# First-batch k and v loads in four 64x64 quarters, paired q tails, and two parameter rows spread by DMA, in a fused attention and MLP kernel

## The chip, the cores and the metric

The kernel runs on one core of one Trainium2 chip. The metric is the device time of one execution in microseconds. Engines are named as in the profile: PE (matrix products), ACT, DVE and POOL (elementwise work), SP (here only the issue of DMAs).

## The reference

Linear attention without a softmax over 8 batches, 8 heads, 576 rows and head size 64, an RMS norm per head, then a mixing block over tokens and channels (width 512, hidden width 2048):

```python
kv = einsum('bhsd,bhse->bhde', k, v)
out = einsum('bhsd,bhde->bhse', q, kv)
x = out / sqrt(mean(out * out, -1) + 1e-6) * g_norm      # heads are then put side by side: (8, 576, 512)
a1 = alpha1 * x + beta1
u = x + lam * einsum('ts,bsd->btd', w_tok, a1)           # token mix
a2 = alpha2 * u + beta2
y = u + lam * (relu(a2 @ w_ch1) @ w_ch2)                 # channel mix
```

All inputs and the output are float32.

## The kernel before

The work of a batch is cut into chunks of 128 rows (four, and a tail of 64). For each batch PE makes k-v products (L674, L684), q-kv products (L765 and L390), the token mix (L854, tails L876), the first channel product (L988 for even batches, L1002 for odd ones, 16 groups with a relu on ACT, L979) and the second (L1024). Between q-kv and token mix stands the norm: a square on ACT (L800), then on DVE a reduce (L802), a reciprocal (L808), a scaling of the result in PSUM (L821) and a product that makes the token mix's operand `rt`, or `rtt` for the tail (L825); POOL multiplies by g_norm (L829).

The first batch is done in another way, in fp32 straight from the loaded tiles, so that PE can start before everything is split into bf16 pairs: k-v products at L610 (`kv_first`), q turned by PE at L632 (main part) and L646 (the 64-row tails), both in `qt_first`, and q-kv products at L772, all in two halves of four heads. L906 is its token mix in halves. The loads of that batch (`load_first` for k and v, L510; L494 and L501 for q) stand first on SP's queue, then w_tok (L1118), the first-matrix weights (L1240) mixed with batch 1's k, v and q, and the second-matrix weights (L1263), one after the other (`P.chain`).

The weights of the second matrix are multiplied by lambda when they are cast (L1269, on DVE or POOL), so `lam_bc`, lambda on all 128 partitions, must be there by then. `a2_bc`, alpha2 on all partitions, is used from the third batch on. These, `e1g_bc` (alpha1 times lambda times g_norm) and `g_bc` are made by a matmul with a row of ones (L1096, `spread`) and a copy.

No engine's order is written by hand. Every operation is recorded with an estimated cost, and for DMAs a transfer time (`dma_us`); `plan` then simulates the queues and fixes each engine's order, choosing priorities so that the first 16 first-channel groups come early. Until the first of them starts, PE gets a filling matmul (L1330, `warm`) wherever the plan finds nothing ready; their number and places are fixed with the order. PSUM has eight banks, which the plan hands out too; a q-kv group of two chunks takes two neighbouring ones until DVE has scaled it. So a changed cost or operation can move instructions anywhere.

Of the kernel before, what the change touches and what calls it, by code (L numbers as in the profile page):

```python
# [17 lines left out]
DM = 512  # L18
# [30 lines left out]
class Prog:  # L49
# [119 lines left out]
    def schedule(self):  # L169
# [226 lines left out]
def bass_transnormer_attn__then__resmlp_affine_kernel(  # L396
# [15 lines left out]
    with ExitStack() as stack:  # L412
# [80 lines left out]
        def load_main(tile, key, src, b, hs, eng="SP"):  # L493
            P.op(eng, 0.6, lambda e: e.dma_start(  # L494
                tile[:, hs].rearrange("p h c d -> p h (c d)"),
                src[b, hs, 0:512, :].rearrange("h (p c) d -> p h (c d)", c=4)),
                w=[(key, a) for a in range(hs.start // 4, hs.stop // 4)],
                dma_us=3.6 * (hs.stop - hs.start) / 8)

# [8 lines left out]
        def load_first(a):  # L508
            for key, src, tile in (("kf", k, kf), ("vf", v, vf)):
                P.op("SP", 0.6, lambda e, src=src, tile=tile: e.dma_start(  # L510
                    six(tile, a).rearrange("p h c d -> p h (c d)"),
                    src[0, HALVES[a], :, :].rearrange("h (p c) d -> p h (c d)", c=6)),
                    w=[(key, a)], dma_us=2.05)

        def load_kv(b, go=()):
            j = (b + 1) % 2
            for tile, tl, src, n in ((kf, kft, k, "kf"), (vf, vft, v, "vf")):
                P.op("SP", 0.6, lambda e, tile=tile, src=src: e.dma_start(
                    tile[:, j].rearrange("p h c d -> p h (c d)"),
                    src[b, :, 0:512, :].rearrange("h (p c) d -> p h (c d)", c=4)),  # L520
                    r=go, w=[(n, j)], dma_us=3.6)
# [77 lines left out]
        def kv_first():  # L599

            def group(a):
                t = P.ptile(1)

                def f(e):
                    ks, vs = six(kf, a), six(vf, a)
                    for c in range(6):
                        for h in range(4):
                            o = t.flat(slice(64 * (h % 2), 64 * (h % 2) + 64))[
                                :, 64 * (h // 2):64 * (h // 2) + 64]
                            m = e.matmul(o, ks[:, h, c, :], vs[:, h, c, :],  # L610
                                         start=(c == 0 and h < 2), stop=(c == 5),
                                         skip_group_check=True)
                    return m
                P.op("PE", 1.7, f, r=[("kf", a), ("vf", a)], w=[t])
                for h in range(2):
                    rows = slice(64 * h, 64 * h + 64)
                    P.op("ACT", act_us(128), lambda e, h=h, rows=rows: copy(
                        e, kv32[rows, 2 * a:2 * a + 2, 64 * h:64 * h + 64],
                        t.flat(rows)[:, 0:128].rearrange("p (r e) -> p r e", r=2)),
                        r=[t, "kvz"], w=[("kv32", a, h)])  # L620
            for a in range(2):
                yield lambda a=a: group(a)

        def qt_first():

            def pair(pr):
                t = P.ptile(1)

                def f(e):
# [5 lines left out]
                    return m  # L635
                P.op("PE", 1.0, f, r=["ident", ("qf", pr // 2)], w=[t])
                P.op(act_dve(512), 0, lambda e: copy(e, qt32[:, pr, 0:512], t.flat()),
                     r=[t], w=[("q32", pr)])

            def tail(a):  # L640
                t = P.ptile(1)

                def f(e):
                    for pr in range(2):
                        for h in range(2):
                            m = e.matmul(t.flat(slice(64 * h, 64 * h + 64))[  # L646
                                :, 64 * pr:64 * pr + 64], qft[0:64, 4 * a + 2 * pr + h, :],
                                ident[0:64, 0:64], start=True, stop=True)
                    return m
                P.op("PE", 0.4, f, r=["ident", "qft0"], w=[t])  # L650
                P.op(act_dve(128), 0, lambda e: copy(
# [362 lines left out]
        def ch2_groups(b):  # L1014
# [31 lines left out]
            for c, n in order:  # L1046
# [4 lines left out]
        abr = xtl[0:8, 1, 64:192]  # L1051
        params = ((moe_lam, prow[:, 512:1024], lam_bc, "lam"),
                  (moe_alpha1, prow[:, 0:512], e1g_bc, "e1"), (g_norm, prow2[:, 0:64], g_bc, "g"),
                  (moe_beta1, prow[:, 1024:1536], None, "e2"),
                  (moe_alpha2, prow[:, 1536:2048], a2_bc, "a2"))

# [9 lines left out]
        def load_params():  # L1066
            t = P.ptile(1)
            P.op("PE", 0.1, lambda e: e.transpose(t.flat()[:, 0:8], abr[0:8, :], ident[0:8, 0:8]),
                 r=["ident", ("abr", 0), ("abr", 1)], w=[t])
            P.op("DVE", 0.2, lambda e: e.tensor_copy(  # L1070
                out=ab2[:].rearrange("p i j -> p (i j)"), in_=t.flat()[:, 0:8]),
                r=[t], w=[("ab2", 0)])
            P.op("DVE", 0.2, lambda e: e.tensor_copy(out=b2c[:], in_=t.flat()[:, 4:8]),
                 r=[t], w=["b2c"])
            e1r, lamr, e2r, gr = (params[i][1] for i in (1, 0, 3, 2))
# [11 lines left out]
            spread(("e1", "g"))  # L1087

        def spread(names):
            late = [] if "g" in names else [("wtm", sc) for sc in range(5)]  # L1090
            for src, row, dst, key in params:
                if key not in names:
                    continue
# [3 lines left out]
                    t.flat()[:, 0:n], ones[:], row, start=True, stop=True),  # L1097
                    r=["ones", key + "r"] + late, w=[t])
                P.op(act_dve(n), 0, lambda e, dst=dst, t=t, n=n: copy(
                    e, dst[:], t.flat()[:, 0:n]), r=[t], w=[key])  # L1100

        def free_rows():
            for kk in (xkeys(1, c) for c in range(4)):
                for x_ in kk:
                    for key in ("e1r", "lamr", "e2r", "a2r"):
                        P.readers.setdefault(x_, []).extend(P.readers[key] + P.lastw[key])
# [113 lines left out]
        run([wt_groups()])  # L1220
        spread(("lam", "a2"))
        free_rows()
# [57 lines left out]
        load_q(1)  # L1280
        load_w(3)
        P.chain = False
        for key in ("wst", "wst2", "hsu"):
# [8 lines left out]
        for i in range(4, 8):  # L1292
            load_w(i)
        P.chain = False

# [67 lines left out]
```

## Time and profile before

| | us |
|---|---|
| median of 3 runs | 373.29 |
| lowest and highest | 373.05, 374.56 |
| profiled execution, its own time | 372.88 |
| its span in the profile | 371.1 |
| PE busy in the span | 359.2 (97%) |
| DVE, ACT, POOL busy | 197.0, 166.2, 79.9 |

The mean granted PE clock is 0.999. All times in the rows below are microseconds from the start of the span unless marked ns. A row of the timeline gives start, length, engine, line, operation, result and operands, shapes, a count of instructions, and in brackets how long the engine was idle before and what ended that. An fp32 matmul appears as two records. The chain of waits is the work that ended last, followed backwards. A row of the table by stretches gives the length, the busy time and count of PE, PEld (weight loads), DVE, ACT and POOL, then the granted clock, the DMA share and GB/s. Transfers stay in flight after the SP row that issued them. Matmuls overlap, so several PE rows together are timed from start to start.

### The profile page before, as it was taken

How to read it: one execution, taken by the hardware profiler on the slowest of the kernel's cores; microseconds unless marked ns; L12 is line 12 of the kernel's file. 1: busy time of each engine (PE TensorE's matmuls, PEld its weight loads, DVE VectorE, ACT ScalarE, POOL GpSimd, SP SyncE). 2: the span in 40 equal slices, each digit the busy share in tenths (PEclk: the TensorE clock that was granted, in tenths of full speed). 3: DMA queues.
4: the chain of work that ended last, by engine and by line, in shares of the span. 5: the costliest groups of instructions: out<-in, count | busy, mean ns of one | idle time of the engine just before them, and what ended most of it. 6: DMA issues, size and time to landing. Idle time of an engine off the chain costs nothing.

```text
span 371.1 us, 6911 instructions
## 1 busy us (share of the span) xinstructions
PE 359.2 (97%) x3074; PEld 208.9 (56%) x2838; DVE 197.0 (53%) x300; ACT 166.2 (45%) x268; POOL 79.9 (22%) x69
## 2 busy tenths in 40 slices
PE   7999999999999999999999999999999999999995
PEld 3887665466654554457664554457654554457642
DVE  3267598976566467834836166924833175720021
ACT  1466797217862088206670087207730186007500
POOL 4046008520242005300242006200520006100000
PEclk9999999999999999999999999999999999999999
DMA  8999999989969399439923399423503110330021
GB/s 191 252 349 296 327 384 300 265 195 253 282 130 226 110 300 225 54 115 260 245 51 86 127 306 185 76 101 58 113 8 107 58 30 1 66 114 5 2 83 58
DMA packets 92456, 59.33 MB, mean 160 GB/s; under 512 B 59454, under 2 KB 83526, under 8 KB 92298
## 3 DMA queue, kind: packets, MB, share of 16 engines
q1 hardware_dynamic: 92400, 58.88, 63.1%
q8 instruction: 23, 0.38, 0.4%
q14 instruction: 7, 0.06, 0.0%
q10 hardware_dynamic: 26, 0.01, 0.0%
HBM read 38.04 MB, written 9.44 MB: 128 GB/s over the span
## 4 chain that ended last, share of the span: by engine, by line
PE 88%; DMA 4%; DVE 4%; ACT 1%; issue 1%; SPq 1%
PE ps L1024 30%; PE ps L1002 18%; PE ps L988 14%; PE ps L854 8%; PE ps L674 4%; DMA qf<-in_q_dram 4%; PE ps L390 2%; PE ps L765 2%; PE ps L876 1%; PE ps L906 1%; PE ps L941 1%; DVE small L802 1%; DVE rt L825 1%; PE ps L684 1%; SPq L510 1%
## 5 line engine op out<-in xcount | busy, mean ns | idle before, releaser
L1024 PE MATMUL ps<-w,ht 128*128 128x512 bf16 x551 | 126.0, 379 | 2.5 <-issue 1.7
L979 ACT ACTIVATE ht<-ps,hb 128x512 bf16<-128x512 f32 (+1 forms) x128 | 93.4, 742 | 46.0 <-PE ps L1002 38.8
L1024 PEld LDWEIGHTS ps<-w,ht 128*128 128x128 bf16 x576 | 54.5, 98 | 64.1 <-issue 1.2
L829 POOL TENSOR_TENSOR xm<-xm,g_bc 128x512 f32<-128x512 f32 (+1 forms) x36 | 46.4, 1288 | 190.3 <-DVE rt L825 188.4
L1002 PE MATMUL ps<-a2t,w 128*128 128x320 bf16 x512 | 72.0, 299 | 0.5 <-ACT ht L979 0.5
L1002 PEld LDWEIGHTS ps<-a2t,w 128*128 128x128 bf16 x512 | 49.2, 98 | 21.6 <-ACT ht L979 1.3
L988 PE MATMUL ps<-a2t,w 128*128 128x512 bf16 x246 | 57.0, 379 | 0.6 <-issue 0.2
L1033 DVE TENSOR_TENSOR xm<-ps,xm 128x512 f32<-128x512 f32 x32 | 22.1, 689 | 63.6 <-PE ps L1024 63.4
L701 ACT ACTIVATE kvd<-ps 64x128 bf16<-64x128 f32 x28 | 7.6, 272 | 86.0 <-PE ps L684 85.6
L988 PEld LDWEIGHTS ps<-a2t,w 128*128 128x128 bf16 x256 | 23.9, 98 | 26.3
L802 DVE TENSOR_REDUCE small<-sq 128x16 f32<-128x1024 f32 (+3 forms) x27 | 25.3, 936 | 23.6 <-ACT sq L800 23.6
L861 DVE TENSOR_TENSOR xm<-ps,xm 128x1024 f32<-128x1024 f32 x14 | 17.0, 1220 | 21.8 <-PE ps L854 21.8
L854 PE MATMUL ps<-rt,wt 128*128 128x512 bf16 x106 | 27.5, 379 | 0.4 <-DVE rtt L825 0.2
L800 ACT ACTIVATE sq<-ps 128x1024 f32<-128x1024 f32 (+3 forms) x27 | 21.6, 798 | 6.7 <-PE ps L772 3.5
L562 DVE TENSOR_TENSOR qs<-qf,qs 128x2048 bf16<-128x2048 f32 (+1 forms) x10 | 16.4, 1659 | 9.4 <-ACT qs L490 9.3
L706 DVE TENSOR_TENSOR kvd<-ps,kvd 64x128 bf16<-64x128 f32 x28 | 8.1, 289 | 25.0 <-ACT kvd L701 24.4
L765 PEld LDWEIGHTS ps<-kvd,qt 128*128 128x128 bf16 x280 | 17.9, 98 | 4.2
L821 DVE TENSOR_TENSOR xm<-ps,small 128x1024 f32<-128x1024 f32 (+1 forms) x18 | 19.7, 1098 | 0.4
L825 DVE TENSOR_TENSOR rt<-xm,e1g_bc 128x1024 bf16<-128x1024 f32 (+1 forms) x17 | 19.4, 1140 | 0.2
L490 ACT ACTIVATE qs<-qf 128x2048 bf16<-128x2048 f32 (+1 forms) x8 | 12.7, 1588 | 14.9 <-DMA qf<-in_q_dram 12.3
L390 PE MATMUL ps<-kvd,qt 128*128 128x64 bf16 x280 | 19.2, 193 | 0.0
L765 PE MATMUL ps<-kvd,qt 128*128 128x64 bf16 x280 | 19.1, 193 | 0.0
(107 smaller groups left out, 293.0 us busy)
## 6 DMA issues: line engine op xcount, KB each, us to landing
out_dram<-xm SPq DMA_DIRECT2D x32, 256.0 KB, 2.4
kf<-in_k_dram SPq DMA_DIRECT2D x7, 1024.0 KB, 9.5
vf<-in_v_dram SPq DMA_DIRECT2D x7, 1024.0 KB, 7.3
qf<-in_q_dram SPq DMA_DIRECT2D x7, 1024.0 KB, 8.7
stg<-in_moe_w_ch_dram SPq DMA_DIRECT2D x3, 1024.0 KB, 12.3
kf<-in_moe_w_ch_dram SPq DMA_DIRECT2D x2, 1024.0 KB, 14.5
kf<-in_k_dram SPq DMA_DIRECT2D x2, 576.0 KB, 8.4
vf<-in_v_dram SPq DMA_DIRECT2D x2, 576.0 KB, 10.4
```

The costliest lines, as they stand in the source:

```text
L390: return pe.add_instruction(mybir.InstMatmult(start_tensor_calc=start, stop_tensor_calc=stop, tile_size=(128, 128), tile_position=(0, 0), ...
L765: e.matmul(o, w, kvd[:, h, 0, :], start=True, stop=False)
L800: P.op("ACT", act_us(64 * m), lambda e: e.activation(sqv, raw(), ACT.Square), r=[t], w=[("sq", sqs)])
L802: P.op("DVE", dve_us(64 * m), lambda e: e.tensor_reduce(out=smv, in_=sqv.rearrange("p (h d) -> p h d", h=m), axis=AX.X, op=ALU.add), r=[(" ...
L825: lambda e: e.tensor_tensor(out=r_, in0=x, in1=eb, op=ALU.mult),
L829: P.op("POOL", pool_us(64 * nh), lambda e, xc=xc: e.tensor_tensor(out=xc, in0=xc, in1=g_bc[rows, None, :].to_broadcast([nr, nh, DH]), op=A ...
L854: m = e.matmul(t.ap()[:, i, :], tok_w(b, sc, c), rsrc(b, sc), start=(sc == 0), stop=(sc == 4))
L979: P.op("ACT", act_us(n) + 0.09, lambda e: e.activation(dst, src(), ACT.Relu, bias=hb[:, fj:fj + 1]), r=[t, ("hb", fj // 4)], w=[("ht", fj)])
L988: m = e.matmul(t.flat(), w1[:, dj, 128 * fj:128 * fj + 128], a2t[:, dj, 0:512], start=(dj == 0), stop=(dj == 3))
L1002: m = e.matmul(t.ap()[:, i, 0:320], w1[:, dj, 128 * fj:128 * fj + 128], a2t[:, dj, 320 * i:320 * i + 320], start=(dj == 0), stop=(dj == 3))
L1024: m = e.matmul(t.flat(), ht[:, fj, 128 * c:128 * c + 128], w2[:, fj, :], start=(fj == 0), stop=(fj == 15))
L1033: P.op("DVE", dve_us(512), lambda e: e.tensor_tensor(out=x, in0=t.flat(), in1=x, op=ALU.add), r=[t] + keys, w=keys)
```

## The change

1. The first batch's k and v. A half of four heads was one DMA onto 96 partitions of 6 rows; it becomes two DMAs of two heads each onto partitions 0 to 63 and 64 to 127, with 9 rows (2304 bytes) to a partition. The k-v products of a half then are 36 matmuls of 64x64, spread over the four quarters of PE, instead of 24 of 96x64.
2. The q tails of the first batch: two heads are turned at once by one transpose, four in all instead of eight matmuls.
3. lambda and alpha2 are spread over the partitions by a DMA that reads the row 128 times, instead of by PE (L1096) and a copy on ACT. The lambda load stands on SP's queue behind the fourth weight load, the alpha2 load behind the eighth. The small row load of alpha2 goes away.
4. Costs that the plan uses are changed: 4.2 instead of 3.6 us for a q load, 3.8 instead of 3.6 for a batch's k or v, 0.6 instead of 0.3 from issue to start of a transfer, and PE times of the operations above.

```diff
-                        dma_free = max(dma_free, t + 0.3) + pick.lat
+                        dma_free = max(dma_free, t + 0.6) + pick.lat
...
-        def six(tile, a):
-            return tile[0:96, a].rearrange("p h c d -> p (h c d)")[:, 0:1536].rearrange(
-                "p (h c d) -> p h c d", h=4, c=6)
+        def nine(tile, a, g):
+            return tile[64 * g:64 * g + 64, a].rearrange("p h c d -> p (h c d)")[
+                :, 0:1152].rearrange("p (h c d) -> p h c d", h=2, c=9)
...
         def load_first(a):
             for key, src, tile in (("kf", k, kf), ("vf", v, vf)):
-                P.op("SP", 0.6, lambda e, src=src, tile=tile: e.dma_start(
-                    six(tile, a).rearrange("p h c d -> p h (c d)"),
-                    src[0, HALVES[a], :, :].rearrange("h (p c) d -> p h (c d)", c=6)),
-                    w=[(key, a)], dma_us=2.05)
+                for g in range(2):
+                    P.op("SP", 0.45, lambda e, src=src, tile=tile, g=g: e.dma_start(
+                        nine(tile, a, g).rearrange("p h c d -> p h (c d)"),
+                        src[0, 4 * a + 2 * g:4 * a + 2 * g + 2].rearrange(
+                            "h (p c) d -> p h (c d)", c=9)),
+                        w=[(key, a)] if g == 0 else [(key + "g", a)], dma_us=1.05)
...
-                t = P.ptile(1)
-                    for c in range(6):
-                        for h in range(4):
-                            o = t.flat(slice(64 * (h % 2), 64 * (h % 2) + 64))[
-                                :, 64 * (h // 2):64 * (h // 2) + 64]
-                            m = e.matmul(o, ks[:, h, c, :], vs[:, h, c, :],
-                                         start=(c == 0 and h < 2), stop=(c == 5),
-                                         skip_group_check=True)
+                t = P.ptile(2)
+                    for c in range(9):
+                        for h in (0, 2, 1, 3):
+                            g, r = h // 2, slice(64 * (h % 2), 64 * (h % 2) + 64)
+                            m = e.matmul(t.ap(r)[:, g, 0:64], nine(kf, a, g)[:, h % 2, c, :],
+                                         nine(vf, a, g)[:, h % 2, c, :],
+                                         start=(c == 0), stop=(c == 8), skip_group_check=True)
...
-                        for h in range(2):
-                            m = e.matmul(t.flat(slice(64 * h, 64 * h + 64))[
-                                :, 64 * pr:64 * pr + 64], qft[0:64, 4 * a + 2 * pr + h, :],
-                                ident[0:64, 0:64], start=True, stop=True)
+                        h = 4 * a + 2 * pr
+                        m = e.transpose(t.flat()[:, 64 * pr:64 * pr + 64],
+                                        qft[0:64, h:h + 2, :].rearrange("p h d -> p (h d)"),
+                                        ident[0:64, 0:64])
...
+        def spread_load(src, dst, key):
+            P.op("SP", 0.6, lambda e: e.dma_start(dst[:], src[None, :].to_broadcast([128, DM])),
+                 w=[key], dma_us=0.9)
...
-        spread(("lam", "a2"))
...
         load_w(3)
+        spread_load(moe_lam, lam_bc, "lam")
...
             load_w(i)
+        spread_load(moe_alpha2, a2_bc, "a2")
```

In the diff `HALVES` are the two halves of four heads, `P.op(engine, cost, function, r=reads, w=writes, dma_us=transfer)` records an operation, and `P.ptile(n)` asks for n banks of PSUM.

More of the change, by code (lines that the diff above doesn't have):

```diff
@@ L497, in load_main @@
                 w=[(key, a) for a in range(hs.start // 4, hs.stop // 4)],
-                dma_us=3.6 * (hs.stop - hs.start) / 8)
+                dma_us=4.2 * (hs.stop - hs.start) / 8)
         def load_tail(tile, key, src, b, lo, eng="SP"):
@@ L520, in load_kv @@
                     src[b, :, 0:512, :].rearrange("h (p c) d -> p h (c d)", c=4)),
-                    r=go, w=[(n, j)], dma_us=3.6)
+                    r=go, w=[(n, j), (n + "g", j)], dma_us=3.8)
                 for g in range(2):
@@ L635, in f @@
                     return m
-                P.op("PE", 1.0, f, r=["ident", ("qf", pr // 2)], w=[t])
+                P.op("PE", 0.95, f, r=["ident", ("qf", pr // 2)], w=[t])
                 P.op(act_dve(512), 0, lambda e: copy(e, qt32[:, pr, 0:512], t.flat()),
@@ L1066, in load_params @@
         def load_params():
-            t = P.ptile(1)
-            P.op("PE", 0.1, lambda e: e.transpose(t.flat()[:, 0:8], abr[0:8, :], ident[0:8, 0:8]),
-                 r=["ident", ("abr", 0), ("abr", 1)], w=[t])
+            ta = P.ptile(1)
+            P.op("PE", 0.1, lambda e: e.transpose(ta.flat()[:, 0:8], abr[0:8, :], ident[0:8, 0:8]),
+                 r=["ident", ("abr", 0), ("abr", 1)], w=[ta])
             P.op("DVE", 0.2, lambda e: e.tensor_copy(
[L1071 to L1074, printed above, removed]
+                out=ab2[:].rearrange("p i j -> p (i j)"), in_=ta.flat()[:, 0:8]),
+                r=[ta], w=[("ab2", 0)])
+            P.op("DVE", 0.2, lambda e: e.tensor_copy(out=b2c[:], in_=ta.flat()[:, 4:8]),
+                 r=[ta], w=["b2c"])
             e1r, lamr, e2r, gr = (params[i][1] for i in (1, 0, 3, 2))
@@ L1086, in load_params @@
                     r=["lamr", "e2r", "rtt0"], w=[("rtt1", i)])
-            spread(("e1", "g"))
-        def spread(names):
-            late = [] if "g" in names else [("wtm", sc) for sc in range(5)]
             for src, row, dst, key in params:
-                if key not in names:
+                if dst is None:
                     continue
@@ L1097, in spread @@
                     t.flat()[:, 0:n], ones[:], row, start=True, stop=True),
-                    r=["ones", key + "r"] + late, w=[t])
+                    r=["ones", key + "r"], w=[t])
                 P.op(act_dve(n), 0, lambda e, dst=dst, t=t, n=n: copy(
@@ L1104, in free_rows @@
                 for x_ in kk:
-                    for key in ("e1r", "lamr", "e2r", "a2r"):
+                    for key in ("e1r", "lamr", "e2r"):
                         P.readers.setdefault(x_, []).extend(P.readers[key] + P.lastw[key])
```

12 lines of the change are left out of this document (5 added, 7 removed).

## The prediction

> **What bounds the kernel now.** I read the page first, then a table of busy time by stage, then the chain that ended last, then the timeline of single stages.
>
> ```profile
> PE 359.2 (97%) x3074; PEld 208.9 (56%) x2838; DVE 197.0 (53%) x300; ACT 166.2 (45%) x268; POOL 79.9 (22%) x69
> DMA  8999999989969399439923399423503110330021
> ```
> ```profile
> 9.00:19.25 10.25, 9.12 (x167) 7.87 (x167) 3.12 (x9) 4.55 (x12) 0.00 (x0) 1.00 1.11 265
> 19.25:42.36 23.11, 22.74 (x270) 18.55 (x274) 14.34 (x31) 14.87 (x30) 9.97 (x12) 1.00 1.08 318
> 42.36:80.00 37.64, 37.05 (x326) 20.17 (x292) 32.81 (x48) 22.53 (x39) 15.58 (x9) 1.00 1.04 301
> ```
>
> PE is busy for 359.2 of 371.1 us. In the table the first numbers are a stage's length and PE's busy time; the last are the granted clock (1.00), the DMA share and GB/s. PE lacks 1.13 us between 9.00 and 19.25, 0.37 up to 42.36 (where the first channel-mix group, L988, starts) and 0.59 up to 80. So only what shortens PE's list, or makes PE wait, can move the end; the DMA queue, full for the first 70 us, counts where PE waits for it. PE's list also holds L1330, a matmul that only fills time: its number is fixed when the program is built, so it runs even when what it bridges is already there.
>
> ```profile
> 9.00 1.62 PE L610 MATMUL ps<-vf,kf 96*64 96x64 f32 x48
> 10.55 1.12 PE L1096 MATMUL ps<-xm,ones 1*128 1x512 f32 x2
> 13.50 0.68 PE L646 MATMUL ps<-ident,qft 64*64 64x64 f32 x16
> 14.11 0.43 PE L1096 MATMUL ps<-xtl,ones 1*128 1x64 f32 x2
> 14.38 0.17 PE L1068 MATMUL ps<-ident,xtl 8*128 8x8 f32 x1
> 19.25 1.97 PE L632 MATMUL ps<-ident,qf 128*64 128x128 f32 x32 [0.62 <-DMA qf<-in_q_dram]
> 21.04 1.04 PE L772 MATMUL ps<-kvd,qt 128*64 128x128 f32 x8
> ```
> ```profile
> 22.24 0.59 PE ps L1330 x2
> 22.83 1.78 PE ps L772 x16
> ...
> 25.10 0.68 PE ps L1177 x5
> ...
> 32.69 1.05 PE ps L1096 x2
> ...
> 37.34 1.05 PE ps L1096 x2
> ...
> 41.81 0.39 PE ps L684 x16
> 42.20 0.16 issue
> 42.36 0.81 PE ps L988 x3
> ```
>
> The second half of q lands at 19.2 and PE has waited 0.62 us for it. From there PE is full: the two spreads of lambda and alpha2 (L1096, 1.05 us each) stand on its path.
>
> **The change, stage by stage**, along the order of the changed program's instructions.
>
> Up to the first k-v group. The changed PE list has 26 fillers instead of 25 in front of it, and the g spread among them. A filler costs 0.216 us (from the L1024 row below: 51 matmuls of the same shape in 11.39 us, less the last one's own 0.38). The g spread takes 0.27 (14.11 to 14.38). So this group starts at 9.0+0.22+0.27, near 9.45, if its loads are there.
>
> From there to the second half of q. A k-v group is now 36 matmuls in 64x64 quarters, 72 records as fp32 goes through twice. The nearest row is L684, fp32 64x64 matmuls in the same four quarters: 0.39 us for 16 records, so 1.76 us, against 1.55 (9.00 to 10.55): +0.21 for each of two groups. The q tails become four transposes; five such take 0.68 (L1177), so 0.54 against 0.61. The g spread is gone from here (-0.27). Half of the tails' q-kv work (L772, 1.04 us for x8) now comes here: +0.5. Three fillers stand here instead of one: +0.43. The busy 9.12 thus becomes 9.12+0.42-0.07-0.27+0.5+0.43 = 10.13, and with the 0.16 of issue that such stretches show, q's second half is first touched at 9.45+10.13+0.16 = 19.75: 0.5 later than now. It landed at 19.2, so even a faster load brings nothing; this is the cover of the whole load edit.
>
> What the loads cost. Four 576 KB halves and two of q land before that.
>
> ```profile
> 12.00:14.00 2.00, 2.00 (x46) 1.83 (x42) 0.01 (x1) 1.29 (x3) 0.00 (x0) 1.00 1.09 226
> 50.00:52.00 2.00, 2.00 (x37) 1.53 (x35) 1.40 (x4) 2.00 (x4) 0.00 (x0) 1.00 1.04 386
> ```
>
> At 226 GB/s a half (590 kB) takes 2.61 us. Upper end for the new shape: 386, what the full queue moves later, so 1.53 us and q at 15, unused. Lower end: two thirds of 226, as 64 partitions are two thirds of 96: 3.9 us, q at 24.4. I take today's rate, as it is the same queue in the same stage: pieces grow from 1536 to 2304 bytes, while the partitions of one transfer shrink. Four more issues on SP cost some 0.4 us each of its own time while the queue is full, so nothing. The Trainium skill (SBUF — State Buffer, "Door 1: The DMA port swizzle") speaks against this edit: 64 neighbouring partitions reach only half of the write ports, 196 GB/s at 1 MiB, and two transfers to the two halves do not add up. By that figure a half takes 3.0 us. No run here shows it yet; the 96-partition row at 226 neither confirms nor denies it.
>
> From q to the first channel-mix group (23.11 us now). Gone: two spreads, -2.10; half of the tail work, -0.5. Added: fillers, 15 instead of 8, 7 x 0.216 = +1.51. The rest is the same work in another order, and I find its feeders (copies by ACT and DVE) ready in time. So 23.11-1.09 = 22.02, and this group starts at 19.75+22.02 = 41.77 instead of 42.36: **-0.6 us**. Of 2.1 us taken from PE the fillers give back most.
>
> The copies of the spreads go from ACT too (two, about 0.6 us each, off the path). In their place come two loads of 256 KB on SP's queue, lambda ahead of the second-matrix loads (L1263), alpha2 after them, ahead of the third batch's k and v. No row shows a load that repeats one row. Lower bound: 256 KB at 386 GB/s, 0.7 us. Upper bound: 128 pieces of 2 KB one after another, each at a sixteenth of 226 GB/s (0.145 us): 18.6 us. I take 0.7, since what is written is an ordinary 128-partition tile. Queued behind are L1263's loads; DVE's first use of them (51.65 below) had no DMA wait before, and now stands behind two more copies of q that DVE takes from ACT, which covers 0.7.
>
> After the first channel-mix group the order differs. Both 32-record q-kv groups of batch 1 now come before the last four channel-mix groups (now: among them), and its token mix (L854) comes after 28 matmuls of L1024 instead of 52.
>
> ```profile
> 40.38 1.06 ACT L490 ACTIVATE w<-kf 128x1024 bf16<-128x1024 f32 x1 [0.18 <-DMA kf<-in_moe_w_ch_dram]
> 48.37 3.34 ACT L490 ACTIVATE qt<-ps 128x1024 bf16<-128x1024 bf16 x4 [0.41 <-PE ps L585]
> 52.28 0.60 ACT L490 ACTIVATE qt<-ps 128x512 bf16<-128x512 bf16 x1
> 51.65 6.71 DVE L1269 TENSOR_TENSOR w<-stg,lam_bc 128x512 bf16<-128x512 f32 x11
> 52.77 5.31 ACT L979 ACTIVATE ht<-ps,hb 128x512 bf16<-128x512 f32 x9
> 58.63 0.19 PE L390 MATMUL ps<-kvd,qt 128*128 128x64 bf16 x1
> 58.86 1.02 ACT L800 ACTIVATE sq<-ps 128x1024 f32<-128x1024 f32 x1 [0.78 <-PE ps L390]
> 59.92 1.22 DVE L802 TENSOR_REDUCE small<-sq 128x16 f32<-128x1024 f32 x1 [1.56 <-ACT sq L800]
> 61.05 1.69 DVE L1269 TENSOR_TENSOR w<-kf,lam_bc 128x512 bf16<-128x512 f32 x1
> 61.32 11.39 PE L1024 MATMUL ps<-w,ht 128*128 128x512 bf16 x51
> 67.48 1.23 DVE L825 TENSOR_TENSOR rt<-xm,e1g_bc 128x1024 bf16<-128x1024 f32 x1
> 71.17 1.65 DVE L825 TENSOR_TENSOR rtt<-xtl,e1g_bc 64x512 bf16<-64x512 f32 x1
> 72.87 1.04 PE L854 MATMUL ps<-rt,wt 128*128 128x512 bf16 x4 [0.17 <-DVE rtt L825]
> ```
>
> Times from here count from the first channel-mix group (F, now 42.36). PE: the first 32-record group ends at F+16.3 now (58.63); two channel-mix groups fewer stand before it (4 x 0.216 each), so F+14.6, the second at F+15.5. Unhindered, four more groups (3.45) and 28 matmuls (6.05) bring PE to L854 at F+25.0. ACT: it was done with 13 relus at F+15.7 (52.77+5.31). It now has two relus less (0.59 each), two copies of q less (0.84 and 0.60), but two weight casts more (1.06 each): F+15.2 or a little earlier, say F+15.0. DVE: from its reduce to the end of rtt took 12.9 us (59.92 to 72.82), 11.2 without the 1.69 of L1269 that no longer stands in it. Reduce starts after ACT's square, F+15.0+1.07, so rtt is ready at F+27.3, 2.3 us after PE gets there; if rtt keeps clear of POOL (0.7 for half of a 1.23 us row instead of 1.65) and the second rt likewise, at F+25.9. A second limit lies nearby: batch 1's q-kv results hold five of eight PSUM banks, so the last channel-mix groups wait for relus that stand behind the squares on ACT, and L854 can hardly start before F+26.2. So PE loses 1.2 to 2.3 us; I take **+1.7**, less the 0.17 it lost there before. Behind the waiting L854 stands all of PE's list. Later the two lists are the same work in nearly the same order.
>
> Sum: -0.6+1.5 = +0.9. The profiled execution took 372.88 (span 371.1 and 1.78 around it), 0.41 below the median of 373.29; so 373.8 by its own time and **374.2** by the median. An effect under 0.5% (1.9 us) is about what a measurement of this kernel can't tell from no change.
>
> **Rivals.**
> 1. The wait at L854 does not come (ACT and DVE keep up): -0.6-0.17, and another order may also avoid the only other long wait on PE, 0.52 us at 102.6:
>
> ```profile
> 102.63 5.61 PE L1002 MATMUL ps<-a2t,w 128*128 128x320 bf16 x40 [0.52 <-ACT ht L979]
> ```
>    Then 373.29-1.3 = 372.0. For it: PE's waits are that rare now. Against: the ACT sum. 0.17.
> 2. Slower: the pieces jam. PE waits for banks first and then, not at the same time, for rtt, and w2's POOL pieces come late; the loss at L854 is 1.2 plus 2.3 instead of 1.7: +1.8 more, 376.0. It decides once ACT's squares start after F+16. 0.20.
> 3. Slower: half the partitions, half the speed. A quarter then runs at half of 386, 193 GB/s, a half takes 3.06 us, and q lands 4 x 0.45 = 1.8 later, at 21.0; beyond 19.75 PE waits, 1.25: 375.4; at the lower end of the loads (q at 24.4) 378.8. Against: 96 of 128 partitions would by the same measure give 290, and today's rate is 226, so something else limits it. 0.13. This is the rule of the skill's page named above, whose 196 GB/s would give 375.3.
> 4. The lambda load runs serially (18.6 us). L1263's first load, there by 51.65 now, comes 18.6 later, at 70; DVE's five pieces ahead of the reduce (0.61 each, 11 in 6.71) end at 73 instead of about 57, and L854 slides by some 16 us: near 390. 0.05.
> 5. The spreads' PE time is really won, since fillers and order do no harm at all: -2.1-0.5 and q at its old time, 370.7. Against: the fillers are in the program. 0.05.
>
> **How the numbers follow.** Forecast 0.40, rivals 0.17, 0.20, 0.13, 0.05, 0.05. Forecast alone: 373.4 (wait 0.8 us shorter) to 375.0. The range reaches down to rival 1 (372.0, leaving out rival 5 and a little) and up to 377.0, leaving out rival 4 and the worst of 2 and 3. Faster by over 0.5% (below 371.4): rival 5 and a few of rival 1, 0.08. Slower by over 0.5% (above 375.2): most of 2 and 3, all of 4, a little of the forecast, 0.36. Within: 0.56.
>
> **What would show it.** In the profile after: L610 at 9.4 with 72 records in 1.76 us; L632's second group at 19.7 with no DMA wait ahead of it; L988 first at 41.8; a wait of 1 to 2 us of PE at L854 or just before it, put down to DVE rtt or ACT relus; no L1096 of 512 columns but one. A DMA wait ahead of L632 means rival 3; one ahead of L1269 on DVE means rival 4. The forecast is wrong if L988 starts before 41 or after 42.7, or if PE's waits between 42 and 80 stay under 0.8 us or pass 3.

## The result, and the profile after

| | before | after |
|---|---|---|
| median, us | 373.17 | 377.99 |
| lowest and highest (four runs each) | 372.62, 374.56 | 377.90, 378.15 |
| span of the profiled execution | 371.1 | 376.2 |
| PE busy | 359.2 | 364.9 |

The changed kernel is slower: ratio 1.0130, 95% interval 1.0115 to 1.0146. The forecast was 374.2, in a range of 372.0 to 377.0. Lines of the changed kernel are mostly one less than before (L987 is the old L988, L1023 the old L1024, L853 the old L854, L1267 the old L1269).

The table by stretches of the changed kernel, same columns and bounds as in the prediction:

```profile
9.00:19.25 10.25, 10.13 (x210) 7.58 (x209) 4.19 (x11) 4.26 (x10) 0.00 (x0) 1.00 1.07 276
19.25:42.36 23.11, 23.11 (x277) 18.35 (x278) 14.11 (x32) 13.90 (x32) 9.66 (x12) 1.00 1.08 328
42.36:80.00 37.64, 33.67 (x277) 17.44 (x235) 34.96 (x44) 22.15 (x36) 16.44 (x10) 0.95 0.76 238
```

Up to 42.36 PE lacks almost nothing. In the third stretch it is busy for 33.67 instead of 37.05 us, and at a mean granted clock of 0.95. The loss shows there. Now the timeline of the changed kernel, first PE's rows ahead of that stretch, which the prediction forecast, then the stretch itself with the rows of all engines that make the chain:

```profile
9.72 1.28 PE L610 MATMUL ps<-vf,kf 64*64 64x64 f32 x72
10.93 1.12 PE L1095 MATMUL ps<-xm,ones 1*128 1x512 f32 x2
19.70 1.97 PE L631 MATMUL ps<-ident,qf 128*64 128x128 f32 x32
41.35 3.63 PE L987 MATMUL ps<-a2t,w 128*128 128x512 bf16 x16
52.38 8.18 POOL L1267 TENSOR_TENSOR w<-stg,lam_bc 128x512 bf16<-128x512 f32 x5 [18.09 <-DMA stg<-in_moe_w_ch_dram]
53.70 7.41 DVE L1267 TENSOR_TENSOR w<-stg,lam_bc 128x512 bf16<-128x512 f32 x5
56.37 1.96 ACT L799 ACTIVATE sq<-ps 128x1024 f32<-128x1024 f32 x2
61.03 2.33 DVE L801 TENSOR_REDUCE small<-sq 128x16 f32<-128x1024 f32 x2
62.27 0.31 ACT L804 ACTIVATE small<-small,eps 128x16 f32<-128x16 f32 x1 [3.37 <-DVE small L801]
63.22 0.69 ACT L978 ACTIVATE ht<-ps,hb 128x512 bf16<-128x512 f32 x1
63.96 1.89 PE L987 MATMUL ps<-a2t,w 128*128 128x512 bf16 x4 [3.97 <-ACT ht L978]
65.64 6.75 PE L1023 MATMUL ps<-w,ht 128*128 128x512 bf16 x28
70.28 1.65 DVE L824 TENSOR_TENSOR rtt<-xtl,e1g_bc 64x512 bf16<-64x512 f32 x1
71.97 3.32 DVE L1267 TENSOR_TENSOR w<-stg,lam_bc 128x512 bf16<-128x512 f32 x2
72.23 1.03 PE L853 MATMUL ps<-rt,wt 128*128 128x512 bf16 x4
75.21 4.63 DVE L1267 TENSOR_TENSOR w<-kf,lam_bc 128x512 bf16<-128x512 f32 x4
69.20 7.22 POOL L828 TENSOR_TENSOR xm<-xm,g_bc 128x512 f32<-128x512 f32 x4 [8.64 <-DVE rt L824]
79.88 2.35 DVE L860 TENSOR_TENSOR xm<-ps,xm 128x1024 f32<-128x1024 f32 x2
81.15 1.05 PE L875 MATMUL ps<-rt,wt 128*64 128x512 bf16 x8
```

Read it as a chain. POOL starts on products of w2 with lambda (L1267) at 52.38, DVE at 53.70, and the two are at it together. DVE's five take 7.41 us, 1.48 each; before, eleven took 6.71, 0.61 each (the next starts a little before one ends; a single one lasts 0.69). Batch 1's squares were done by ACT at 58.33, but DVE comes to reduce them (L801) only at 61.03. ACT stands at L804, which needs the reduction, for 3.37 us, and relus (L978) are queued behind it. PE's last channel-mix group needs the PSUM bank that such a relu must free: it stands still for 3.97 us. After that the granted clock falls, in the table of busy time by short stretches (here length, PE's busy time and count, clock, DMA share, GB/s):

```profile
64.00:66.00 2.00, 2.00 (x5) 0.50 1.13 269
66.00:68.00 2.00, 2.00 (x9) 0.82 1.13 297
```

At half the clock the group's four matmuls take 1.68 us from start to start (0.87 in the first experiment) and the 28 of L1023 6.59 (6.08 in the fifth): another 1.3 us (0.8 and 0.5). Later DVE's six remaining products (7.95 us) stand beside POOL's L828, and the token mix's addition L860, which before began at 75.24, begins at 79.88. PE, late by then itself, shows no wait for it: L875 in the last row has no bracket.

From the first channel-mix group to the first of batch 1's (L1001) there were 43.58 us before (42.36 to 85.94) and are 49.47 now (41.35 to 90.82): +5.9, of which 4.0 is the wait and 1.3 the clock. The 0.6 that is left stands in no wait of the trace. Ahead of the first group 1.0 us was won. Together +4.9, which is the difference of the spans (5.1) but for 0.2. The clock's 1.3 us are those of the profiled execution: one of the four timed runs had a mean clock of 1.000 and took 377.98 all the same, and no trace of that one is there to say why.

### The profile page after: what moved, and what is told of

Same layout as the page of the kernel before. It is cut to its first block, busy times and chain, and to the rows that moved or that the text cites. A ratio compares the mean times of both kernels' runs of the same rounds, so it can differ in the third digit from the quotient of the medians.

```text
span 376.2 us, 7047 instructions
## 1 busy us (share of the span) xinstructions
PE 364.9 (97%) x3161; PEld 208.7 (55%) x2881; DVE 202.3 (54%) x298; ACT 165.1 (44%) x268; POOL 81.1 (22%) x69
## 4 chain that ended last, share of the span: by engine, by line
PE 89%; DVE 8%; ACT 1%; issue 1%
PE ps L1023 31%; PE ps L1001 18%; PE ps L987 12%; PE ps L853 7%; PE ps L673 4%; DVE w L1267 4%; PE ps L1330 3%; PE ps L764 2%; PE ps L390 2%; PE ps L875 1%; PE ps L771 1%; PE ps L905 1%; PE ps L940 1%; DVE small L801 1%; PE ps L631 1%; DVE xm L820 1%
## 5 line engine op out<-in xcount | busy, mean ns | idle before, releaser
L1023 PE MATMUL ps<-w,ht 128*128 128x512 bf16 x576 | 131.1, 380 | 0.0
L978 ACT ACTIVATE ht<-ps,hb 128x512 bf16<-128x512 f32 (+1 forms) x128 | 93.2, 742 | 46.7 <-PE ps L1001 40.1
L828 POOL TENSOR_TENSOR xm<-xm,g_bc 128x512 f32<-128x512 f32 (+1 forms) x36 | 50.0, 1388 | 203.7 <-DVE rt L824 201.9
L1023 PEld LDWEIGHTS ps<-w,ht 128*128 128x128 bf16 x576 | 54.7, 98 | 64.9 <-issue 2.7
L1001 PE MATMUL ps<-a2t,w 128*128 128x320 bf16 x512 | 72.2, 299 | 0.0
L987 PE MATMUL ps<-a2t,w 128*128 128x512 bf16 x256 | 59.7, 383 | 4.5 <-ACT ht L978 4.3
L1001 PEld LDWEIGHTS ps<-a2t,w 128*128 128x128 bf16 x512 | 49.5, 98 | 20.8 <-ACT ht L978 0.3
L987 PEld LDWEIGHTS ps<-a2t,w 128*128 128x128 bf16 x256 | 23.9, 98 | 32.2 <-ACT ht L978 5.4
L801 DVE TENSOR_REDUCE small<-sq 128x16 f32<-128x1024 f32 (+3 forms) x27 | 25.1, 932 | 25.3 <-ACT sq L799 25.2
L860 DVE TENSOR_TENSOR xm<-ps,xm 128x1024 f32<-128x1024 f32 x14 | 17.0, 1221 | 24.3 <-PE ps L853 24.2
L853 PE MATMUL ps<-rt,wt 128*128 128x512 bf16 x112 | 28.7, 379 | 0.0
L853 PEld LDWEIGHTS ps<-rt,wt 128*128 128x128 bf16 x112 | 11.0, 98 | 12.7
```

The costliest lines, as they stand in the source:

```text
L801: P.op("DVE", dve_us(64 * m), lambda e: e.tensor_reduce(out=smv, in_=sqv.rearrange("p (h d) -> p h d", h=m), axis=AX.X, op=ALU.add), r=[(" ...
L828: P.op("POOL", pool_us(64 * nh), lambda e, xc=xc: e.tensor_tensor(out=xc, in0=xc, in1=g_bc[rows, None, :].to_broadcast([nr, nh, DH]), op=A ...
L853: m = e.matmul(t.ap()[:, i, :], tok_w(b, sc, c), rsrc(b, sc), start=(sc == 0), stop=(sc == 4))
L978: P.op("ACT", act_us(n) + 0.09, lambda e: e.activation(dst, src(), ACT.Relu, bias=hb[:, fj:fj + 1]), r=[t, ("hb", fj // 4)], w=[("ht", fj)])
L987: m = e.matmul(t.flat(), w1[:, dj, 128 * fj:128 * fj + 128], a2t[:, dj, 0:512], start=(dj == 0), stop=(dj == 3))
L1001: m = e.matmul(t.ap()[:, i, 0:320], w1[:, dj, 128 * fj:128 * fj + 128], a2t[:, dj, 320 * i:320 * i + 320], start=(dj == 0), stop=(dj == 3))
```

## The experiments

Theory A: DVE and POOL get in each other's way in w2's products, and the place of these products in the plan is what costs the time. Theory B: the new order of PE's groups does it by itself, through PSUM banks and relus. Theory C: the edits' own instructions and loads do it. The recorded expectations call POOL GpSimd. Each ratio is against runs of the kernel before on the same chip, whose medians lay between 373.05 and 373.29. The experiments are numbered in the order of their runs and told by subject.

**First: POOL without its reads.** The order of every engine stays; the five blocks of w2 that POOL made hold zeros.

```diff
-  op(dve_pool(512), 0, lambda e, hh=hh: e.tensor_tensor(out=w2[...], in0=s_[:, hh], in1=lam_bc[:], op=ALU.mult), ...)
+  op(dve_pool(512), 0, lambda e, hh=hh: e.memset(w2[...], 0.0) if e is nc.gpsimd
+     else e.tensor_tensor(out=w2[...], in0=s_[:, hh], in1=lam_bc[:], op=ALU.mult), ...)
```

> The changed kernel with one thing taken out: the five of its sixteen w2 products (w2 = staged weights times lambda) that GpSimd computes are replaced on GpSimd by a memset of the same 128x512 block, so GpSimd still writes but no longer reads SBUF there; these five blocks of w2 hold zeros. The order of every engine is unchanged. Theory A (DVE's and GpSimd's products take turns at reading SBUF, so DVE's five pieces ahead of the batch-1 norm take 7.4 us instead of 3.4): DVE's five pieces take 0.69 us each, its first norm reduction starts near 57.4 instead of 61.0, PE's 4.0 us wait ahead of the last channel-mix group falls under 1.5, and the time is 372.5 to 375. Theory B (the order itself: the last channel-mix groups wait for PSUM banks held by batch 1's five q-kv results and for relus queued behind the squares on ACT, whatever DVE does): the pieces get short, but the wait of about 4 us stays and the time stays at 377 to 378.

Measured: 374.78, ratio 1.0041 (1.0026 to 1.0057). 3.2 us of the 4.8 are gone. Its timeline (DVE's products have line L1268 here):

```profile
54.04 3.10 DVE L1268 TENSOR_TENSOR w<-stg,lam_bc 128x512 bf16<-128x512 f32 x5
54.05 1.11 POOL L1267 MEMSET w<- 128x512 bf16 x2 [19.43 <-DMA stg<-in_moe_w_ch_dram]
57.77 2.35 DVE L801 TENSOR_REDUCE small<-sq 128x16 f32<-128x1024 f32 x2 [0.63 <-ACT sq L799]
60.83 1.04 PE L987 MATMUL ps<-a2t,w 128*128 128x512 bf16 x4 [0.49 <-ACT ht L978]
61.70 6.21 PE L1023 MATMUL ps<-w,ht 128*128 128x512 bf16 x28
68.73 1.04 PE L853 MATMUL ps<-rt,wt 128*128 128x512 bf16 x4 [0.83 <-DVE rtt L824]
```

POOL works on writes alone, and DVE's five take 3.10. A memset is also shorter than a product (0.52 us against 1.27 to 1.8), so the experiment takes away some of POOL's time together with its reads. That the reads count, and not that POOL works at all, rests on the two DVE products that ran beside the first two memsets: 0.69 and 0.68 us. PE's wait falls from 3.97 to 0.49 us in the same order with the same banks, so theory B does not hold for the larger part. PE now comes early enough to wait for rtt (0.83).

**Fifth: POOL's other reader too.** As the first, and batch 1's product by g on POOL (L828) becomes a memset of zeros.

> The first experiment's kernel with one more of GpSimd's readers taken out: its product of batch 1's normed tile by the gain g (five instructions between 66 and 75) becomes a memset of the same block. Batch 1's residual and five blocks of w2 are zeros; the order of all engines stays. Theory A (what was left of the loss in the first experiment, 1.5 us, is DVE's last six w2 products taking turns with this GpSimd work, 7.96 us instead of 4.1, ahead of the token mix's additions): these six run at 0.69 us, the transposes of batch 1 come 3 us earlier, and the time falls from 374.8 to 373 to 374. Theory B (the remaining 1.5 us is the order: PE waits for DVE's norm chain ahead of the token mix): 374.4 to 375.2, no change.

Measured: 373.17, ratio 1.0004 (0.9994 to 1.0014): the loss is gone.

```profile
66.92 0.69 DVE L824 TENSOR_TENSOR rtt<-xtl,e1g_bc 64x512 bf16<-64x512 f32 x1
67.64 1.29 DVE L1269 TENSOR_TENSOR w<-stg,lam_bc 128x512 bf16<-128x512 f32 x2
68.85 2.49 DVE L1269 TENSOR_TENSOR w<-kf,lam_bc 128x512 bf16<-128x512 f32 x4
67.67 1.04 PE L854 MATMUL ps<-rt,wt 128*128 128x512 bf16 x4
```

The last six products take 3.78 instead of 7.95 us, rtt 0.69 instead of 1.65, and PE comes to the token mix without a wait. With that the whole slowdown is laid to DVE's and POOL's products side by side, in two places. Taken away in this order they give back 3.2 us for the first and 1.6 us for the second; the second costs PE something only once the first is cured. Here too the memsets are shorter than the products (L828's four take 2.30 us instead of 7.22), and rtt ran beside them in 0.69 us.

**Second: all products on DVE.** `dve_pool(512)` in L1267 becomes DVE alone; the plan is made anew.

> The changed kernel with all sixteen w2 products offered to DVE alone; the plan is made anew (the number of fillers, 45, and the place of batch 1's q-kv groups ahead of the last channel-mix groups stay). Theory A (taking turns): no DVE product takes over 0.75 us outside GpSimd's other work, PE's wait between 55 and 66 falls under 1.5 us, and the time is 372.5 to 375 although DVE has five more pieces (3.4 us). Theory B (order and PSUM banks): PE still waits some 4 us there and the time is 376.5 to 378.

Measured: 377.93, ratio 1.0126 (1.0102 to 1.0149). The time that theory A gave was missed; it lies in theory B's range, but the wait of 4 us that B gave is not there.

```profile
65.02 2.36 DVE L824 TENSOR_TENSOR rt<-xm,e1g_bc 128x1024 bf16<-128x1024 f32 x2
66.33 7.20 POOL L828 TENSOR_TENSOR xm<-xm,g_bc 128x512 f32<-128x512 f32 x4 [30.90 <-DVE rt L824]
69.08 8.48 DVE L1267 TENSOR_TENSOR w<-stg,lam_bc 128x512 bf16<-128x512 f32 x7
69.11 1.04 PE L853 MATMUL ps<-rt,wt 128*128 128x512 bf16 x4 [2.81 <-DVE rtt L824]
80.00 1.23 DVE L860 TENSOR_TENSOR xm<-ps,xm 128x1024 f32<-128x1024 f32 x1
```

The first place is cured (no product of DVE ahead of the norm takes over 0.69 us, and the wait before the last channel-mix groups is 0.92), but the plan now puts the token mix after 16 matmuls of L1023 instead of 28, so PE waits 2.81 us for rtt, and eleven products are left for the time beside L828, where seven take 8.48 us. The first channel-mix group also comes 1.1 us later (42.49). To take work from POOL does not help when the rest falls into POOL's other work.

**Third, fourth, seventh, eighth: the change in parts.** Part 4's PE times go with the operations that they belong to. Third: the changed kernel with part 3 undone:

```diff
-        spread_load(moe_lam, lam_bc, "lam")
-        spread_load(moe_alpha2, a2_bc, "a2")
+        spread(("lam", "a2"))
```

Fourth: the kernel before with the three DMA costs of part 4 alone; seventh: the changed kernel with the three old ones (the same three lines turned round):

```diff
-                        dma_free = max(dma_free, t + 0.3) + pick.lat
+                        dma_free = max(dma_free, t + 0.6) + pick.lat
...
-                dma_us=3.6 * (hs.stop - hs.start) / 8)
+                dma_us=4.2 * (hs.stop - hs.start) / 8)
...
-                    r=go, w=[(n, j)], dma_us=3.6)
+                    r=go, w=[(n, j)], dma_us=3.8)
```

Eighth: the kernel before with parts 1 and 2 alone, as the diff of the change has them (`nine` for `six`, `e.transpose` for the tails).

> The changed kernel with part 3 undone: lambda and alpha2 are again spread by two matmuls of PE, not by a load; quarters, q tails and the planner's costs stay as changed. The plan gives 36 fillers instead of 45, twelve of sixteen w2 products on DVE first and GpSimd only the last four, as before the change. Theory A: DVE's first products run at 0.69 us, the norm reduction starts by 58, and in spite of 2.1 us of spreads back on PE the time is 371.5 to 374.5. Theory C (the quarter loads and 72-record groups themselves cost the time): 376 to 379, with the loss ahead of the first channel-mix group.

> The kernel before with nothing but the planner's three DMA costs changed as in the change (issue 0.3 to 0.6, loads 3.6 to 4.2 and 3.6 to 3.8): the same instructions, another order. The plan puts six w2 products on GpSimd and both q-kv groups of batch 1 together ahead of the last channel-mix groups, as in the changed kernel. Theory A and theory B alike (what costs is the order that the plan makes, not the edits): 375 to 379, with a wait of PE of 3 us or more between 55 and 66. Theory C (the edits themselves cost it): 372.5 to 374.

> The changed kernel with the planner's three old DMA costs (0.3, 3.6, 3.6): quarters, q tails and loaded spreads stay. The plan again gives five early w2 products to GpSimd and now puts all five q-kv groups of batch 1 in one block ahead of the last channel-mix groups; 39 fillers. Theory A: DVE's first four products take 1.2 to 1.8 us each, PE waits 3 to 5 us between 55 and 68, 376.5 to 379.5. Theory C (the new costs in the planner are what lost the time): 372 to 374.

> The kernel before with parts 1 and 2 only: quarter loads of k and v with their 72-record groups, and q tails turned by pairs; spreads by PE and old planner costs. The plan gives five early w2 products to GpSimd beside five of DVE, 24 of the last channel-mix matmuls behind three of five q-kv groups; 30 fillers. Theory A: DVE's products before the norm slow down to over 1.2 us each and the time is 374 to 378, though no edit touches this stage. Theory C (only the edits' own instructions count): 372.5 to 374.

| | us | ratio, interval | w2 products of DVE before the norm, each | longest wait of PE between 42 and 80 |
|---|---|---|---|---|
| third: parts 1, 2, 4 | 372.99 | 0.9994 (0.9985 to 1.0003) | 12, 0.61 | under 0.2 |
| fourth: costs alone | 378.81 | 1.0153 (1.0124 to 1.0182) | 4, 1.69 | 4.02 |
| seventh: parts 1, 2, 3 | 378.33 | 1.0142 (1.0121 to 1.0164) | 4, 1.58 | 3.67 |
| eighth: parts 1, 2 | 376.69 | 1.0102 (1.0078 to 1.0126) | 3, 1.57 | 1.99 |

All four times lie in the ranges that theory A gave. In the eighth the 1.99 us stand ahead of the token mix (L853), for DVE's rt; in the fourth and seventh the wait is that of the changed kernel, ahead of the last channel-mix groups. Timeline of the fourth, which has no new instruction at all:

```profile
53.89 7.97 POOL L1269 TENSOR_TENSOR w<-stg,lam_bc 128x512 bf16<-128x512 f32 x5 [1.44 <-DMA stg<-in_moe_w_ch_dram]
53.99 6.75 DVE L1269 TENSOR_TENSOR w<-stg,lam_bc 128x512 bf16<-128x512 f32 x4
63.59 4.45 PE L988 MATMUL ps<-a2t,w 128*128 128x512 bf16 x12 [4.02 <-ACT ht L979]
```

Three numbers in a simulation make the kernel before 5.6 us slower, in the same way as the change does; and three parts of the change together, in a plan where POOL comes only near the end of DVE's twelve, cost nothing. Theory C is out: the edits' own instructions decide neither sign. In these four, what goes with the loss is whether DVE's products ahead of the norm run beside POOL's. It is not the only place where time can be lost: in the second experiment POOL had no product of w2 at all.

**Sixth: lambda earlier.** One line of the changed kernel moved:

```diff
         load_w(0)
+        spread_load(moe_lam, lam_bc, "lam")
         load_w(1)
...
         load_w(3)
-        spread_load(moe_lam, lam_bc, "lam")
```

> The changed kernel with lambda's load moved from behind the last first-matrix load to behind the first of them. All else as changed. The plan now gives 12 of 16 w2 products to DVE ahead of the norm, GpSimd only the last four, and the token mix of batch 1 after 56 matmuls of the second channel matrix, as before the change; 49 fillers. Theory A (the loss is where the w2 products stand, which the late lambda decided): no wait of PE over 1.5 us between 42 and 80, 371.5 to 374. Theory B (batch 1's q-kv groups ahead of the last channel-mix groups cost it by PSUM banks): 376 to 378, with PE's wait of some 4 us kept. A delay of the first channel-mix loads by the 256 KB (0.7 us at 386 GB/s) may show ahead of the first channel-mix group.

Measured: 373.62, ratio 1.0016 (1.0006 to 1.0026).

```profile
42.68 3.40 PE L987 MATMUL ps<-a2t,w 128*128 128x512 bf16 x15 [0.16 <-issue]
53.12 7.31 DVE L1267 TENSOR_TENSOR w<-stg,lam_bc 128x512 bf16<-128x512 f32 x12
60.28 5.33 POOL L1267 TENSOR_TENSOR w<-kf,lam_bc 128x512 bf16<-128x512 f32 x4 [24.02 <-DMA kf<-in_moe_w_ch_dram]
```

Twelve products at 0.61 us, POOL comes as the last of them ends, and 4.4 us are back with all four parts of the change in place. No wait on PE over 0.2 us is left between 42 and 80. The channel-mix group comes 1.3 us later than in the changed kernel; four more fillers (49 for 45) are 0.9 of that.

**Twelfth: POOL comes later.** In the changed kernel, after the plan is made (`w2_ops` collects the products):

```diff
+        on = {e: sorted((o for o in w2_ops if o.eng == e), key=lambda o: o.start) for e in ("DVE", "POOL")}
+        on["POOL"][0].deps.add(on["DVE"][1])
```

> The changed kernel with every engine's order kept and one wait added: GpSimd's first w2 product waits for DVE's second one, so that GpSimd comes to its five products in the middle of DVE's run of five instead of 1.3 us ahead of it. Nothing is left out. Theory A1 (as in the kernel before, where GpSimd's product came in the middle of DVE's run and took 3.87 us: DVE keeps its pace to the end of the run): DVE's five products take 3.1 us, GpSimd's first takes over 2 us, the norm reduction starts near 57.7, PE's wait ahead of the last channel-mix groups falls under 1 us, 374.3 to 376. Theory A2 (the two take turns whenever both have work): DVE's last three products take 1.7 us each, the run about 6.3 us, the reduction starts near 60, and the time is 376.5 to 378.

Measured: 376.60, ratio 1.0094 (1.0077 to 1.0111).

```profile
53.94 5.26 DVE L1269 TENSOR_TENSOR w<-stg,lam_bc 128x512 bf16<-128x512 f32 x5
55.36 7.66 POOL L1269 TENSOR_TENSOR w<-stg,lam_bc 128x512 bf16<-128x512 f32 x5 [20.84 <-DVE w L1269]
62.06 1.04 PE L987 MATMUL ps<-a2t,w 128*128 128x512 bf16 x4 [1.82 <-ACT ht L978]
```

DVE's last two products take 1.77 and 1.76, the first three 0.69 or less: the engines take turns as soon as POOL is there, so theory A1 falls here. A2 is right in kind and was off by one product (POOL came during the third). With runs of five of 3.10, 5.26 and 7.41 us, PE's waits before the last channel-mix group are 0.49, 1.82 and 3.97, and the times 374.78, 376.60 and 377.99: the dose goes with the effect.

**Ninth to eleventh: the fillers.** Part 3 was to free 2.1 us of PE, and the plan put more fillers in. Here the orders stay, but each filler after the first k-v group's reads 64 columns instead of 512: 22 of them in the sixth experiment's kernel, nine in the third's, nine in the kernel before.

```diff
+            count[0] += 1
+            if count[0] > 27:      # 25 in the kernel before
+                return e.matmul(t.flat()[:, 0:64], wz[:, 0:128], wz[:, 0:64], start=True, stop=True)
             return e.matmul(t.flat(), wz[:, 0:128], wz, start=True, stop=True)
```

> The sixth experiment's kernel (all of the change, lambda's load earlier) with the same order on every engine, but the 22 fillers behind the first k-v group's 27 read 64 columns instead of 512. Theory D (fillers stand on PE's path and give back what the removed spreads free): each saves about 0.19 us, the first channel-mix group comes at 38.5 to 40.5 instead of 42.7, and the time is 369.5 to 372. Theory E (fillers only cover waits for feeders and loads that are really there): PE shows these waits instead, the group stays within 0.7 us of 42.7, and the time at 373 to 374.

> The third experiment's kernel (quarters, q tails and new planner costs, spreads by PE) with the same order, but the nine fillers behind the first k-v group's 27 read 64 columns instead of 512. Theory D: 9 times 0.19, 1.7 us less: 371 to 371.8. Theory E: 372.5 to 373.3.

> The kernel before with the same order, but the nine fillers behind the first 25 read 64 columns instead of 512; nothing of the change in it. Theory D: 1.7 us less than before: 371.2 to 372. Theory E: 372.7 to 373.5, unchanged. If this one and the kernel with the spreads on PE gain alike, quarters and tails are worth nothing by themselves.

| | us | ratio to before | gained on its own base |
|---|---|---|---|
| ninth, on the sixth | 371.77 | 0.9959 (0.9946 to 0.9972) | 1.9 (base 373.62) |
| tenth, on the third | 371.39 | 0.9953 (0.9941 to 0.9965) | 1.6 (base 372.99) |
| eleventh, on the kernel before | 372.24 | 0.9973 (0.9962 to 0.9984) | 1.1 (base 373.29) |

Timelines, first of the ninth and then of the eleventh; they differ in what comes late next:

```profile
36.90 1.09 PE L940 MATMUL ps<-ident,xm 128*128 128x128 f32 x8 [1.12 <-DVE xm L922]
40.61 3.40 PE L987 MATMUL ps<-a2t,w 128*128 128x512 bf16 x15 [0.16 <-issue]
```
```profile
19.73 1.97 PE L632 MATMUL ps<-ident,qf 128*64 128x128 f32 x32 [0.81 <-DMA qf<-in_q_dram]
42.11 1.67 PE L988 MATMUL ps<-a2t,w 128*128 128x512 bf16 x7 [0.16 <-issue]
```

In the ninth the channel-mix group comes 2.07 us earlier (42.68 in the sixth), not 22 times 0.19, 4.2: the other fillers covered waits, of which one for DVE (1.12) now shows. In the eleventh the wait for q grows from 0.62 to 0.81, and q's second half is touched at 19.73 instead of 19.25, so this profiled execution won only 0.25 by the group. It was the slowest of the seven timed ones (372.65, which is 0.23 under the profiled one before); the median won 1.1. In the tenth, with its quarter loads, the group comes at 40.63 after 41.99 and no wait for q shows. So theory D holds in part in all three: 1.9 of 4.2, 1.6 of 1.7 and 1.1 of 1.7 us. The eleventh came out between the ranges of D and E. The ninth and the tenth, with most of the change in them, beat the kernel before by 1.5 and 1.9 us. The eleventh, with nothing of the change, beats it by 1.05: the tenth lies 0.85 below it, so that much comes with quarters, tails and the new order once the fillers are small. Which of these brings it was not separated.

## Why the prediction was wrong

**Up to the first channel-mix group it held.** The first k-v group was forecast for 9.45 and came at 9.72; q's second half was touched at 19.70 (19.75 forecast) without a DMA wait; the channel-mix group came at 41.35 (41.77 forecast), and at 41.80 to 41.92 in three experiments with the same PE order. The length of a k-v group was oversized: the first 72 records took 1.21 us (9.72 to 10.93) against 1.76 forecast, which makes the group shorter than the old 48 (1.55), not longer. The second took 1.64 (17.52 to 19.16), with a stop of about 0.3 in its middle. That 19.70 agrees with the forecast to 0.05 is luck in part: the first group started 0.27 late and was 0.55 short. Rival 3 did not come: no DMA wait ahead of L631. Between 12 and 14, where both kernels load the second half of k and v, the new shape kept the rate that the prediction took (226 GB/s in its row). Busy time by stretches of the changed kernel, the last column GB/s:

```profile
12.00:14.00 2.00, 2.00 (x35) 1.83 (x35) 0.00 (x0) 1.20 (x3) 0.00 (x0) 1.00 1.06 221
```

The Trainium skill's figure (SBUF — State Buffer, "Door 1: The DMA port swizzle"), 196 GB/s for 64 partitions, is exceeded by the 221 of the changed kernel's queue, so it did not bind here. The quarters made the loads neither faster nor slower in that stretch. Rival 4 did not come: DVE shows no DMA wait ahead of L1267, POOL's was for `stg`.

**The step that failed** is the sum after the first channel-mix group, in its DVE term: it lets the reduction follow ACT's square at once and puts nothing for the five products of w2 that DVE has ahead of it. ACT's squares came at F+15.0, to the tenth as forecast (56.37 less 41.35). But the reduction, forecast for F+16.1, came at F+19.7, and rtt was ready at F+30.6 instead of F+27.3. The only price that the prediction names for the five products (in rival 4) is 0.61 each, the pace of a run that POOL had hardly touched; they took 1.48 each. It had the warning in its own rows: L1269 once at 1.69, and rtt at 1.65 where 0.7 was its share. It put this down to POOL for rtt alone, and did not ask how many products the new plan gives to POOL early (five, against one before). So the wait was sized 1.7 and measured 3.97, and in the profiled execution 1.3 us of clock came with it, for which the sum had no term. The place and the party named for the wait, ACT's relus ahead of L853, were right.

Rival 2 had PE's wait for banks right, and a wrong condition: it was to decide when the squares start after F+16, and they started at F+15.0. What was late were DVE's products of w2, not POOL's. Rivals 1 and 5 are refuted for this kernel. That fillers give back what the spreads free was borne out, in the part that the ninth to eleventh experiments show.

The Trainium skill (SBUF — State Buffer, "Who interferes with whom") states the rule that was missing in the sum: a DVE instruction with two SBUF inputs contends with a POOL instruction that reads SBUF, not with one that only writes. The changed kernel and the first experiment show the two halves of it: DVE's products took up to 1.76 us beside POOL's products, and 0.69 and 0.68 beside its memsets.

## What to carry to other kernels

Where a planner orders the engines, a change's own instructions may cost nothing while the order it provokes costs five microseconds: compare which engine gets which elementwise pieces, and what runs beside them, before costing anything. DVE and POOL products with two SBUF operands are to be counted as one engine's time, 1.7 us for a pair here, and are best placed where nobody waits for the next step of either. A filler of fixed number gives back what is saved ahead of it, so it has to be trimmed when the work around it shrinks.

## What the runs showed of the hardware

- In the profiled executions a wait of 3.97 us on PE was followed by a granted clock of 0.50 for 2 us or more, and so were 4.02 and 3.67 us in the fourth and seventh experiments; one of 2.81 us in the second was followed by none (a row by stretches after it, below; the clock is the third number from the end). The Trainium skill (TensorE: Matmul & The Clock Gate, "Part 1: The HAM clock gate (the "warmup" mystery)") gives half clock after an idle window of about 3.4 us; these traces agree. The length of the wait may not decide alone: one of the second experiment's four runs had a mean clock of 0.995, the others 0.999.

```profile
70.00:72.00 2.00, 2.00 (x11) 0.94 (x10) 2.00 (x2) 0.79 (x1) 1.84 (x3) 1.00 0.17 43
```

- Taking turns is not all. In the kernel before, POOL came to one product in the middle of DVE's run of eleven, and that product ended only 1.1 us after the run did (a product of POOL alone takes 1.27):

```profile
55.62 3.87 POOL L1269 TENSOR_TENSOR w<-stg,lam_bc 128x512 bf16<-128x512 f32 x1 [19.51 <-DMA stg<-in_moe_w_ch_dram]
```

  The same shows beside the runs of eleven or twelve in the third, tenth and eleventh experiments (3.15, 2.45 and 3.16 us). In the twelfth experiment POOL came in the middle of a run of five and got its turn at once. What decides between the two was not found.
- The same PE order in four kernels took 5.62 to 6.50 us for the first 18 fillers, and the first k-v group started between 9.61 and 10.49. The first channel-mix group then came between 41.35 and 41.92, and not in the order of the starts (9.61 and 41.82, 9.72 and 41.35), so the start alone does not set it. Between kernels of one PE order the group thus differs by up to 0.57 us.
